# A long convolution with a feed-forward layer: first chunk of k ahead of the filter, bf16 copies in pairs, whole sine tables

## The chip, the core and the metric

The kernel runs on one core of a Trainium2 chip. The metric is the device time of one execution in microseconds (us); lower is better. The core has five engines with a queue each: TensorE (PE in the profile; its weight loads are PEld), VectorE (DVE), ScalarE (ACT), GpSimd (POOL) and SyncE (SP), which issues most DMAs.

## What is computed

```
# q, k, v, x: (1, 2048, 512); shift_k: (512, 4); ssm_k: (512, 2048); all bf16
k_shift = sum over t of k_pad[:, t:t+S, :] * shift_k[:, 3-t]      # four taps per channel
kv  = k_shift * v
y   = irfft(rfft(kv, 2S) * rfft(ssm_k, 2S))[:S] + kv * ssm_D       # long causal convolution
h   = x + layernorm(x) * y                                         # x is q
out = h + relu(layernorm(h) @ w1) @ w2                             # 512 -> 1376 -> 512
```

## The kernel before

The convolution is done as a discrete Fourier transform in two stages of matrix products. Everything up to about 45 us belongs to the part that the change touches; after it come the spectra of the filter and of kv, their product, the inverse transform and the feed-forward layer, with no edit.

**Loads.** SyncE's queue issues `wsh` (the taps), then `sk` (ssm_k, 2 MB, L97), then for each of four chunks of 512 positions a transposing load of k into `kT` (L110) and one of v into `vT` (L111). Each waits its turn in that queue.

**Tables.** GpSimd writes index ramps (L140 to L149). `_turns` (L42) makes of them, in two VectorE instructions, the angles of a table, and a Sin activation on ScalarE makes the table: `cs` (sine, L166) at once, in two instructions of 128x2048, and `cc` (cosine) in slices of four rows, two instructions of 128x256 after each `group_k` (L273). `cn`, the negated sine, is made of `cs` by GpSimd in eight pieces (L192). `f1hi` and `f1lo` are the small first-stage table in two bf16 parts. `wdiag`, made by GpSimd (L195), holds for each channel group and tap a 128x128 matrix with the tap's factors on the diagonal.

**Rows.** `to_rows` (L200) turns eight columns of 128 x 128 with TensorE transposes into one PSUM tile `pst` and copies it (VectorE for D, ScalarE for A, L210 and L208) into `kfl` for ssm_k, later into `xfl` for kv. `pst`, the tap products `pkv` and the first-stage tiles `ps` all come from one ring of eight PSUM slots (tag "ps"): the ninth tile waits until the first is read.

**Rounds.** `taps(u)` (L260) makes the four tap products for chunk u // 4 and channel group u % 4 in one PSUM tile, and VectorE multiplies it with v into `kvx` (L267), which lies in the bytes of `sk`. `stage1` (L213) multiplies rows of `kfl` with `f1hi` and `f1lo` (32-row products, four row groups side by side, 16 quads in a call) and copies the four tiles out. `group_k(gb)` is stage 1 for the filter and a slice of `cc`. The order is written out by hand: `taps(0)`, then seven times `group_k(gb)` and two `taps`, then `taps(15)` and `group_k(7)`. Then `to_rows` makes `xfl` of `kvx`, and eight rounds of `spectrum_k` (twice) and `stage1` on `xfl` follow.

Of the kernel before, what the change touches and what calls it, by code (L numbers as in the profile page):

```python
# [8 lines left out]
ACT = mybir.ActivationFunctionType  # L9
ALU = mybir.AluOpType  # L10
BF16 = mybir.dt.bfloat16
F32 = mybir.dt.float32
F32R = mybir.dt.float32r
I32 = mybir.dt.int32
PSUM = bass.MemoryType.PSUM
P = 128
# [25 lines left out]
def _turns(nc, out, r, col, M, quarter):  # L42

    nc.vector.tensor_scalar(out=out, in0=r, scalar1=col, scalar2=float(M // 2 + (M // 4 if quarter else 0)),
                            op0=ALU.mult, op1=ALU.add)
    nc.vector.tensor_single_scalar(out=out, in_=out, scalar=M - 1, op=ALU.bitwise_and)
# [10 lines left out]
def kernel(  # L57
# [13 lines left out]
    nc = tc.nc  # L71
    _, S, D = A_q.shape
    DFF = B_w1.shape[1]
    KS = A_shift_k.shape[1]
    assert S == 2048 and D == 512 and KS == 4, "kernel is specialised to S=2048, D=512, ks=4"
    NT = 16
    DC = D // P
    NFC = (DFF + P - 1) // P
    x_d, k_d, v_d, out_d = A_q[0], A_k[0], A_v[0], out[0]
# [5 lines left out]
    consts = pl.push("consts")  # L85
    slotA = pl.push("slotA")
    vp = pl.push("vp")
    early = pl.push("early")
    wp = pl.push("wp", side="right")
    kvp = pl.push("kvp", side="right")  # L90
    psum = pl.push("psF", bufs=8, space=PSUM)


    wsh = consts.tile([P, DC, KS], BF16, name="wsh")
    nc.sync.dma_start(out=wsh[:], in_=A_shift_k.rearrange("(r p) j -> p r j", p=P))
    sk = early.tile([P, DC, S], BF16, name="sk")
    nc.sync.dma_start(out=sk[:], in_=A_ssm_k.rearrange("(c p) t -> p c t", p=P))  # L97
    d0 = early.tile([P, DC, 64], BF16, name="d0")
    for dp in range(2):
        src = bass.AP(tensor=A_ssm_D.tensor, offset=A_ssm_D.offset + 64 * dp, ap=[[0, 64], [P, DC], [1, 64]])  # L100
        nc.scalar.dma_start(out=d0[64 * dp:64 * dp + 64, :, :], in_=src)
    CH = 512
    vTs = [vp.tile([P, DC, CH], BF16, name=f"vT{c}") for c in range(4)]
    kT = kvp.tile([P, DC, 16 + S], BF16, name="kT")
    wdiag = kvp.tile([P, DC, KS, P], BF16, name="wdiag")

    nc.vector.memset(kT[:, :, 0:16], 0.0)
    for c in range(4):
        ts = slice(CH * c, CH * c + CH)
        nc.sync.dma_start_transpose(out=kT[:, :, 16 + CH * c:16 + CH * c + CH], in_=k_d[ts, :])  # L110
        nc.sync.dma_start_transpose(out=vTs[c][:], in_=v_d[ts, :])  # L111


    TURN = 2.0 * math.pi * SIN_SHRINK
# [14 lines left out]
    def _sin(out, turns, M, neg=False):  # L129
# [4 lines left out]
    ident = consts.tile([P, P], BF16, name="ident")  # L134
    nc.gpsimd.memset(ident[:], 0.0)
    nc.gpsimd.affine_select(out=ident[:], in_=ident[:], compare_op=ALU.not_equal, fill=1.0,
                            base=0, pattern=[[-1, P]], channel_multiplier=1)
    n2i = early.tile([P, 1], I32, name="n2i")
    for s in range(0, P, 64):
        nc.gpsimd.iota(n2i[s:s + 64, :], pattern=[[0, 1]], base=0, channel_multiplier=1)  # L140
    r2 = early.tile([P, 32, 64], I32, name="w_r")
    nc.gpsimd.iota(r2[:], pattern=[[2, 32], [128, 64]], base=1, channel_multiplier=0)
    n1i = early.tile([P, 1], I32, name="n1i")
    for s in range(0, P, 32):
        nc.gpsimd.iota(n1i[s:s + 32, :], pattern=[[0, 1]], base=0, channel_multiplier=1)
# [1 line left out]
    nc.gpsimd.iota(r1[:], pattern=[[2, 32]], base=1, channel_multiplier=0)  # L147
    r3 = early.tile([P, 64], I32, name="dm_r")
    nc.gpsimd.iota(r3[:], pattern=[[1, 64]], base=0, channel_multiplier=0)  # L149
    n1c = early.tile([P, 1], F32, name="n1c")  # L150
    n2c = early.tile([P, 1], F32, name="n2c")
    nc.vector.tensor_copy(out=n2c[:], in_=n2i[:])


    cc = wp.tile([P, 32, P], F32R, name="c2c")
    cs = wp.tile([P, 32, P], F32R, name="c2s")
    cn = wp.tile([P, 32, P], F32R, name="c2n")

    def table(dst, turns, ks=slice(0, 32)):
        for dp in range(2):  # L160
            nc.scalar.activation(out=dst[:, ks, 64 * dp:64 * dp + 64], in_=turns[:, ks, :], func=ACT.Sin,
                                 scale=hsc[:, dp:dp + 1], bias=hbi[:, dp:dp + 1])

    tsn = early.tile([P, 32, 64], I32, name="w_ts")
    _turns(nc, tsn[:], r2[:], n2c[:], 8192, False)
    table(cs, tsn)  # L166
    nc.vector.tensor_copy(out=n1c[:], in_=n1i[:])

    t1 = early.tile([P, 64], I32, name="f1_t")
    _turns(nc, t1[:, 0:32], r1[:], n1c[:], 128, True)  # L170
# [7 lines left out]
    _turns(nc, t3[:, 1, :], r3[:], n2c[:], 64, False)  # L178
    dsc = early.tile([P, 2, 64], F32, name="dm_f")
    _sin(dsc[:], t3[:], 64)  # L180
    _turns(nc, r2[:], r2[:], n2c[:], 8192, True)
    f1hi = consts.tile([P, 64], BF16, name="f1_hi")
    nc.vector.tensor_copy(out=f1hi[:], in_=f1f[:])
    f1d = early.tile([P, 64], F32, name="f1_d")
# [1 line left out]
    f1lo = consts.tile([P, 64], BF16, name="f1_lo")  # L186
    nc.vector.tensor_copy(out=f1lo[:], in_=f1d[:])

    dtab = consts.tile([P, 8, DC, 8], BF16, name="dtab")
    for h in range(8):  # L190
        hs = slice(4 * h, 4 * h + 4)
        nc.gpsimd.tensor_single_scalar(out=cn[:, hs, :], in_=cs[:, hs, :].bitcast(F32), scalar=-1.0, op=ALU.mult)  # L192
        if h == 0:
            for rg in range(DC):
                nc.gpsimd.tensor_tensor(out=wdiag[:, rg, :, :], in0=ident[:].unsqueeze(1).to_broadcast([P, KS, P]),  # L195
                                        in1=wsh[:, rg, :].unsqueeze(2).to_broadcast([P, KS, P]), op=ALU.mult)
            nc.gpsimd.tensor_copy(out=dtab[:], in_=d0[:].rearrange("p r (o g) -> p o r g", g=8))


    def to_rows(cols, q, fl, eng):  # L200
        pst = psum.tile([P, 8, P], BF16, tag="ps", name="pst")
        for i in range(8):
            nc.tensor.transpose(out=pst[:, i, :], in_=cols(8 * q + i), identity=ident[:])  # L203
        copy(eng, fl[:, :, :, 8 * q:8 * q + 8], pst[:].rearrange("p i (d g) -> p g d i", d=2))

    def copy(eng, o, i):
        if eng == "A":
            nc.scalar.copy(out=o, in_=i)  # L208
        else:
            nc.vector.tensor_copy(out=o, in_=i)  # L210


    def stage1(gb, fl, a_out, engs, parts=1):  # L213
        n = 8 // parts
        for h in range(parts):
            pss = [psum.tile([P, n, 64], F32, tag="ps", name=f"ps1_{r}") for r in range(4)]
            for gi in range(n):
                for f, first in ((f1hi, True), (f1lo, False)):
                    for rg in range(4):
                        rows = slice(32 * rg, 32 * rg + 32)  # L220
                        nc.tensor.matmul(out=pss[rg][:, gi, :],  # L221
                                         lhsT=fl[rows, 8 * gb + n * h + gi, :, :].rearrange("p d n -> p (d n)"),
                                         rhs=f[rows, :], start=first, stop=not first, tile_position=(32 * rg, 0))
            for rg in range(4):
                copy(engs[(4 * gb + rg) % len(engs)], a_out(gb, 8 * rg + n * h, n),
                     pss[rg][:].rearrange("p g c -> p c g"))
# [12 lines left out]
                             skip_group_check=True)  # L239


    kfl = early.tile([P, 64, 2, 64], BF16, name="kfl")
    skv = sk[:].rearrange("p c (a b) -> p c a b", b=64)
    for q in range(8):
        to_rows(lambda n: skv[:, :, :, n], q, kfl, "DADADADA"[q])

    dre = consts.tile([P, 2, P], F32R, name="dre")
    dim = consts.tile([P, 2, P], F32R, name="dim")
# [5 lines left out]
    a1k = a1[:].rearrange("p (c j) -> p c j", j=256)  # L254
    a1x = a1[:].rearrange("p (o c j) -> p o c j", o=8, j=32)


    kvx = sk[:].rearrange("p c t -> p (c t)").rearrange("p (h r a l) -> p h r a l", h=16, r=DC, l=4)

    def taps(u):  # L260
        c, rg = divmod(u, DC)
        ps = psum.tile([P, CH], F32, tag="ps", name="pkv")
        for j in range(KS):
            nc.tensor.matmul(out=ps[:], lhsT=wdiag[:, rg, j, :], rhs=kT[:, rg, CH * c + 16 - j:CH * c + CH + 16 - j],  # L264
                             start=(j == 0), stop=(j == KS - 1))
        split = "p (a h l) -> p a h l"
        nc.vector.tensor_tensor(out=kvx[:, :, rg, 8 * c:8 * c + 8, :].rearrange("p h a l -> p a h l"),  # L267
                                in0=ps[:].rearrange(split, h=16, l=4),
                                in1=vTs[c][:, rg, :].rearrange(split, h=16, l=4), op=ALU.mult)

    def group_k(gb):
        stage1(gb, kfl, lambda o, j, n: a1k[:, :, 32 * o + j:32 * o + j + n], "ADAADADA")
        table(cc, r2, slice(4 * gb, 4 * gb + 4))  # L273

    taps(0)
    for gb in range(7):
        group_k(gb)
        taps(2 * gb + 1)
        taps(2 * gb + 2)
    taps(15)  # L280
    group_k(7)
    for pq in halves:
        for dst, rho, blk, sgn in ((dre, 0, 0, 1.0), (dre, 1, 1, 1.0), (dim, 0, 1, -1.0), (dim, 1, 0, 1.0)):
            nc.gpsimd.tensor_single_scalar(out=dst[pq, rho, pq], in_=dsc[pq, blk, :], scalar=sgn / 2048, op=ALU.mult)
    pl.pop("kvp")
    xfp = pl.push("xfp", side="right")
    xfl = xfp.tile([P, 64, 2, 64], BF16, name="xfl")
    kvc = kvx.rearrange("p h r a l -> p h (r a) l")
    for q in range(8):
        to_rows(lambda n: kvc[:, n // 4, :, n % 4], q, xfl, "ADADADAD"[q])  # L290
    pl.pop("early")
    pl.pop("vp")
    slotB = pl.push("slotB")
# [20 lines left out]
    psum = pl.push("psP", bufs=2, space=PSUM)  # L314
# [69 lines left out]
    psum = pl.push("psI", bufs=8, space=PSUM)  # L384
# [30 lines left out]
    for b in range(32):  # L415
        ps = psum.tile([P, 2, 2 * P], F32, tag="ps", name="psi1")
        m0 = 16 * (b % 4) + 2 * (b // 4)
        for i in range(2):
            m = 2 * b + i
            for c, d in ((0, dre), (1, dim)):  # L420
                nc.tensor.matmul(out=ps[:, i, :], lhsT=kf[:, c, 4 * m:4 * m + 4, :].rearrange("p r k -> p (r k)"),  # L421
                                 rhs=d[:].rearrange("p a b -> p (a b)"), start=(c == 0), stop=(c == 1))
        dst = bp[:, m0:m0 + 2, :, :, :].rearrange("p g a b c -> p g (a b c)")
# [149 lines left out]
    psum = pl.push("psM", bufs=3, space=PSUM)  # L573
# [51 lines left out]
```

## Time and profile before

| | |
|---|---|
| median of 13 runs | 222.65 us (221.7 to 223.8) |
| profiled execution, its time | 223.72 us |
| profiled execution, span on the core | 221.9 us |
| PE busy, share of the span | 198.4 us, 89% |
| DVE busy, share of the span | 149.9 us, 68% |
| ACT busy, share of the span | 132.6 us, 60% |
| POOL busy, share of the span | 72.3 us, 33% |
| granted TensorE clock in every slice of the first 100 us | 1.00 |
| TensorE products of ssm_k's transposes begin | 10.29 us |
| transposes of kvx begin | 38.27 us |

Times in the profile are microseconds from the start of the span unless they are marked ns. In a row of the timeline stand start, length, engine, line, operation, output and inputs, count and in brackets the idle time before it with what ended it. In a row of the groups stand, after the first bar, busy us and mean ns of one instruction, and after the second the engine's idle time before them with its releaser. A q after an engine's name means its queue of DMA issues. The granted clock is the share of TensorE's clock that a throttle let through; the durations show the rest.

### The profile page before, as it was taken

The page shows a single profiled execution, that of the slowest core. Times are in us where ns is not written, and L with a number is a line of the kernel's source. Part 1 is how long each engine was busy: PE and PEld are TensorE (multiplying, and loading weights), DVE is VectorE, ACT ScalarE, POOL GpSimd, SP SyncE. Part 2 cuts the span into 40 slices and gives each one's busy share as a digit, 9 for nine tenths or more (in the row PEclk, how much of TensorE's full clock was granted, in tenths as well). Part 3 has the DMA queues.
Part 4 walks back from the last instruction along what each step waited for, and adds up shares of the span by engine and source line. Part 5 has one row for each costly group of instructions (what it writes and reads, how often), then busy time and mean ns, then how long its engine had stood idle before and what let it go on. Part 6 is the DMA issues. An engine that isn't in the chain of part 4 may idle for free.

```text
span 221.9 us, 7269 instructions
## 1 busy us (share of the span) xinstructions
PE 198.4 (89%) x3092; PEld 137.9 (62%) x3111; DVE 149.9 (68%) x299; ACT 132.6 (60%) x252; POOL 72.3 (33%) x103
## 2 busy tenths in 40 slices
PE   0199699989979999989988799999999999999993
PEld 0194355989968999969976578544444444444452
DVE  4988878989988999966877779751973257130031
ACT  2858967978885888868974879203650066206500
POOL 8399940000018999978300120220022002000000
PEclk9999999999999999999999999999999999999999
DMA  4999940000000000029990000232013110421012
GB/s 154 317 225 195 175 93 4 1 3 6 3 3 3 1 0 3 1 82 227 275 303 9 3 3 3 41 68 63 24 28 80 41 47 4 95 60 38 0 44 53
DMA packets 30384, 15.41 MB, mean 69 GB/s; under 512 B 25520, under 2 KB 29072, under 8 KB 30224
## 3 DMA queue, kind: packets, MB, share of 16 engines
q1 hardware_dynamic: 29520, 14.76, 28.8%
q8 instruction: 24, 0.39, 0.7%
q10 hardware_dynamic: 832, 0.20, 0.4%
q14 instruction: 8, 0.07, 0.1%
HBM read 7.08 MB, written 2.10 MB: 41 GB/s over the span
## 4 chain that ended last, share of the span: by engine, by line
PE 74%; DVE 10%; DMA 5%; issue 4%; ACT 3%; POOL 2%; SPq 1%; DVEq 0%
PE ps2m L540 14%; PE ps1m L528 13%; PE psi L421 7%; PE psy L347 6%; PE pkv L264 6%; PE pz L454 5%; PE pst L203 5%; PE ps L221 4%; DMA sk<-in_A_ssm_k_dram 4%; PE ps2k L236 4%; DVE st L479 4%; PE u L236 4%; PE u L238 3%; PE ps2k L238 3%; POOL rstd L475 2%
## 5 line engine op out<-in xcount | busy, mean ns | idle before, releaser
L530 ACT ACTIVATE h1T<-ps1m 128x512 bf16<-128x512 f32 (+3 forms) x55 | 27.4, 514 | 21.2 <-PE ps1m L528 20.3
L528 PE MATMUL ps1m<-hlnT,w 128*128 128x512 bf16 (+3 forms) x219 | 39.5, 336 | 0.3
L540 PE MATMUL ps2m<-w,h1T 128*128 128x512 bf16 (+3 forms) x177 | 38.9, 366 | 0.7 <-issue 0.3
L542 DVE TENSOR_TENSOR o<-ps2m,xh 128x512 bf16<-128x512 f32 (+1 forms) x17 | 11.1, 659 | 38.1 <-PE ps2m L540 32.8
L528 PEld LDWEIGHTS <-w 128*128 128x128 bf16 (+1 forms) x220 | 21.8, 100 | 17.6 <-issue 1.4
L540 PEld LDWEIGHTS <-h1T 128*128 128x128 bf16 (+1 forms) x187 | 17.6, 98 | 21.2 <-issue 3.1
L337 DVE TENSOR_TENSOR t<-u,kf 128x704 fp32r<-128x704 f32 x32 | 26.7, 886 | 3.0 <-ACT usb L333 2.7
L337 POOL TENSOR_TENSOR t<-usb,kf 128x320 fp32r<-128x320 f32 x32 | 28.2, 919 | 1.3 <-ACT usb L333 1.0
L465 ACT CAST zt<-pz 128x512 bf16<-128x512 f32 x16 | 8.4, 594 | 30.3 <-PE pz L454 30.3
L454 PE MATMUL pz<-bp,ecore 32*32 32x128 f32 x1024 | 23.4, 384 | 2.8 <-issue 1.8
L474 POOL TENSOR_SCALAR rstd<-mv 128x4 f32<-128x4 f32 (+1 forms) x7 | 1.6, 232 | 70.7 <-DVE mv L481 70.7
L208 ACT CAST a<-ps 128x512 fp32r<-128x512 f32 (+1 forms) x38 | 19.4, 569 | 4.6 <-PE ps L221 4.5
L454 PEld LDWEIGHTS pz<-bp,ecore 32*32 32x32 f32 x1024 | 14.5, 103 | 10.5 <-issue 6.3
L210 DVE CAST a<-ps 128x512 fp32r<-128x512 f32 (+1 forms) x30 | 18.4, 651 | 2.4 <-PE ps L221 2.4
L203 PE MATMUL pst<-ident,sk 128*128 128x128 bf16 x128 | 10.1, 248 | 10.5 <-DMA sk<-in_A_ssm_k_dram 10.3
L208 ACT CAST kf<-psy 128x512 fp32r<-128x512 f32 x30 | 17.4, 640 | 1.8 <-PE psy L347 0.3
L479 DVE BATCH_NORM_STATS2 st<-xh 128x6 f32<-128x512 bf16 x28 | 17.3, 676 | 0.0
L264 PE MATMUL pkv<-kT,wdiag 128*128 128x512 bf16 x56 | 14.8, 381 | 2.1 <-issue 1.7
L203 PEld LDWEIGHTS <-sk 128*128 128x128 bf16 x128 | 9.8, 152 | 10.6 <-DMA sk<-in_A_ssm_k_dram 10.3
L421 PE MATMUL psi<-dre,kf 128*128 128x256 f32 x64 | 15.5, 284 | 0.9 <-ACT kf L208 0.9
L347 PE MATMUL psy<-t,ipos 128*128 128x512 f32 x48 | 15.8, 391 | 0.0
L421 PE MATMUL psi<-dim,kf 128*128 128x256 f32 x64 | 15.4, 283 | 0.0
(111 smaller groups left out, 387.4 us busy)
## 6 DMA issues: line engine op xcount, KB each, us to landing
sk<-in_A_ssm_k_dram SPq DMA_DIRECT2D x1, 2048.0 KB, 9.0
out_dram<-o SPq DMA_DIRECT2D x58, 32.0 KB, 1.6
xh<-in_A_q_dram SPq DMA_DIRECT2D x4, 384.0 KB, 6.8
w<-in_B_w_dram SPq DMA_DIRECT2D x1, 1376.0 KB, 12.8
w<-in_B_w_dram SPq DMA_DIRECT2D x1, 1280.0 KB, 15.9
xh<-in_A_q_dram SPq DMA_DIRECT2D x4, 128.0 KB, 2.8
hlnT<-hln SPq DMA_TRANSPOSE x12, 2.4
w<-in_B_w_dram SPq DMA_DIRECT2D x1, 96.0 KB, 15.6
```

What stands on the lines that cost most here:

```text
L203: nc.tensor.transpose(out=pst[:, i, :], in_=cols(8 * q + i), identity=ident[:])
L208: nc.scalar.copy(out=o, in_=i)
L210: nc.vector.tensor_copy(out=o, in_=i)
L264: nc.tensor.matmul(out=ps[:], lhsT=wdiag[:, rg, j, :], rhs=kT[:, rg, CH * c + 16 - j:CH * c + CH + 16 - j], start=(j == 0), stop=(j == KS ...
L337: eng.tensor_tensor(out=t[:, :, j, :], in0=in0.unsqueeze(1).to_broadcast([P, 2, n, 2]), in1=kfr[:, :, j, ks], op=ALU.mult)
L347: nc.tensor.matmul(out=psy[:], lhsT=m_[:], rhs=t_.rearrange("p j k -> p (j k)"), start=first, stop=not first)
L421: nc.tensor.matmul(out=ps[:, i, :], lhsT=kf[:, c, 4 * m:4 * m + 4, :].rearrange("p r k -> p (r k)"), rhs=d[:].rearrange("p a b -> p (a b)" ...
L454: nc.tensor.matmul(out=pz[32 * a:32 * a + 32, r4, l4, :], lhsT=ecore[rows, rho, n2, :], rhs=rhs, start=(rho == 0), stop=(rho == 1), tile_p ...
L479: nc.vector.bn_stats(out=st[:, t % 4, :], in_=xh[:, t, :])
L528: nc.tensor.matmul(out=ps1[:fsz, :], lhsT=w1[:, c, fc * P:fc * P + fsz], rhs=hlnTs[sc][:, c, part], start=(c == 0), stop=(c == DC - 1))
L530: nc.scalar.activation(out=h1s[sc][:fsz, fc, part], in_=ps1[:fsz, :], func=ACT.Relu)
L540: nc.tensor.matmul(out=ps2[:], lhsT=h1s[sc][:ksz, fc, i * P:(i + 1) * P], rhs=w2[:ksz, fc, ds], start=(fc == 0), stop=(fc == NFC - 1))
```

## The change

- k's first chunk is issued ahead of ssm_k, v's first chunk behind it; the other chunks follow in the old order.
- ssm_k loads into a new tile `pre` in slot A, where the angles of the sine table also lie; `kvx` gets a tile of its own.
- Eleven products of a tile of ones are written to a PSUM tile that nobody reads, at the head of TensorE's queue; then `taps` 0 to 3. Their products with v (`times_v`) stand on VectorE behind the second tile of `kfl`.
- `wdiag` moves from GpSimd to VectorE, ahead of the small tables; the long ramp comes last on GpSimd. `cs` is made after the small tables, and `cc` in two whole halves: one ahead of `kfl`'s tiles, one behind them.
- `kfl` and `xfl` hold channels in pairs; `to_rows` copies on VectorE as int32 words with a bitwise or by zero, on ScalarE in two halves; the engine letters change (six of eight tiles on VectorE). Stage 1's weights then have a step of two elements.
- The eight rounds hold twelve `taps`, in turns two and one, ahead of each `group_k`, whose copies go three to ScalarE and one to VectorE ("AADAAADA").

```diff
+    for _ in range(11):
+        nc.tensor.matmul(out=warm[:], lhsT=wz[:, 0:P], rhs=wz[:], start=True, stop=True)
     nc.vector.memset(kT[:, :, 0:16], 0.0)
-    for c in range(4):
+    for c, src in ((0, "k"), (0, "s"), (0, "v"), (1, "k"), (1, "v"), (2, "k"), (2, "v"), (3, "k"), (3, "v")):
...
+    for rg in range(DC):
+        nc.vector.tensor_tensor(out=wdiag[:, rg, :, :], in0=ident[:].unsqueeze(1).to_broadcast([P, KS, P]),
+                                in1=wsh[:, rg, :].unsqueeze(2).to_broadcast([P, KS, P]), op=ALU.mult)
...
-    _turns(nc, r2[:], r2[:], n2c[:], 8192, True)
+    tsn = pre[:, 4096:6144].rearrange("p (k n) -> p k n", n=64)
+    _turns(nc, tsn, r2[:], n2c[:], 8192, False)
+    table(cs, tsn)
...
+    _turns(nc, r2[:], r2[:], n2c[:], 8192, True)
+    table(cc, r2[:], (0,))
...
-        copy(eng, fl[:, :, :, 8 * q:8 * q + 8], pst[:].rearrange("p i (d g) -> p g d i", d=2))
+        qs = slice(8 * q, 8 * q + 8)
+        if eng == "D":
+
+            nc.vector.tensor_single_scalar(out=fl[:].rearrange("p g d n c -> p g d (n c)").bitcast(I32)[:, :, :, qs],
+                                           in_=pst[:].bitcast(I32).rearrange("p i (d g) -> p g d i", d=2),
+                                           scalar=0, op=ALU.bitwise_or)
+        else:
+            for d in range(2):
+                nc.scalar.copy(out=fl[:, :, d, qs, :],
+                               in_=pst[:, :, 64 * d:64 * d + 64].rearrange("p i (g c) -> p g i c", c=2))
...
-                                         lhsT=fl[rows, 8 * gb + n * h + gi, :, :].rearrange("p d n -> p (d n)"),
+                                         lhsT=fl[rows, (8 * gb + n * h + gi) // 2, :, :, gi % 2].rearrange("p d n -> p (d n)"),
...
-        stage1(gb, kfl, lambda o, j, n: a1k[:, :, 32 * o + j:32 * o + j + n], "ADAADADA")
-        table(cc, r2, slice(4 * gb, 4 * gb + 4))
-
-    taps(0)
-    for gb in range(7):
+        stage1(gb, kfl, lambda o, j, n: a1k[:, :, 32 * o + j:32 * o + j + n], "AADAAADA")
+
+    first = [taps(u) for u in range(4)]
+
+    kfl = early.tile([P, 32, 2, 64, 2], BF16, name="kfl")
+    skv = skf.rearrange("p (c a b) -> p c a b", c=DC, b=64)
+    for q in range(8):
+        to_rows(lambda n: skv[:, :, :, n], q, kfl, "DDDDADDA"[q])
+        if q == 1:
+            for u, ps in first:
+                times_v(u, ps)
+    table(cc, r2[:], (1,))
...
+    for gb in range(8):
+        for u in ((4, 5), (6,), (7, 8), (9,), (10, 11), (12,), (13, 14), (15,))[gb]:
+            times_v(*taps(u))
         group_k(gb)
-        taps(2 * gb + 1)
-        taps(2 * gb + 2)
-    taps(15)
-    group_k(7)
...
-        to_rows(lambda n: kvc[:, n // 4, :, n % 4], q, xfl, "ADADADAD"[q])
+        to_rows(lambda n: kvc[:, n // 4, :, n % 4], q, xfl, "DDADDADD"[q])
```

## The prediction

> **What bounds the kernel now.** I read the chain of waits first, in order of time, to see which work ends last in the stretch that the change touches (0 to 45 us of a span of 221.9 us).
>
> ```profile
> 1.25 8.99 DMA sk<-in_A_ssm_k_dram
> 10.29 6.38 PE pst L203 x64
> 16.70 1.02 ACT kfl L208
> 17.77 0.68 PE ps L221 x64
> 18.45 0.32 PE pkv L264
> 18.82 1.46 PE pkv L264 x6
> ...
> 26.12 1.70 issue
> ...
> 38.27 3.77 PE pst L203 x64
> ```
>
> Columns are start, length, what. The kernel does nothing for 10.29 us until ssm_k (sk) has landed, transposes it (64 products), evicts the last tile, and then TensorE sets the pace: a round of `group_k` and two `taps` repeats every 2.45 us (0.61 us for 64 small products of L221, 8 tap products at 0.23 us). At 26.12 TensorE loses 1.70 us in which it waits for nothing that the profile shows. At 38.27 the second set of transposes, of kvx, begins. I call that moment the milestone: everything after it is the same work on the same engines, so what the change gains there it keeps, unless a later step becomes slower. Next the timeline of the first 17 us, for the durations and the order in each queue.
>
> ```profile
> 1.79 8.27 SPq L110 DMA_TRANSPOSE kT<-in_A_k_dram  x1
> ...
> 3.56 2.83 POOL L145 IOTA n1i<- 32x1 int32 x4
> ...
> 6.23 4.08 ACT L161 ACTIVATE c2s<-w_ts,hbi,hsc 128x2048 fp32r<-128x2048 int32 x2 [2.81 <-DVE w_ts L46]
> ...
> 8.20 1.28 DVE L44 TENSOR_SCALAR w_r<-w_r,n2c 128x2048 int32<-128x2048 int32 x1
> 9.52 1.23 DVE L46 TENSOR_SCALAR w_r<-w_r 128x2048 int32<-128x2048 int32 x1
> ...
> 10.11 2.01 SPq L111 DMA_TRANSPOSE vT<-in_A_v_dram  x1
> ...
> 12.28 1.01 ACT L208 COPY kfl<-pst 128x1024 bf16<-128x1024 bf16 x1 [1.24 <-PE pst L203]
> ...
> 13.80 1.01 ACT L208 COPY kfl<-pst 128x1024 bf16<-128x1024 bf16 x1 [0.51 <-PE pst L203]
> ...
> 15.25 1.01 ACT L208 COPY kfl<-pst 128x1024 bf16<-128x1024 bf16 x1 [0.43 <-PE pst L203]
> ...
> 16.70 1.01 ACT L208 COPY kfl<-pst 128x1024 bf16<-128x1024 bf16 x1 [0.44 <-PE pst L203]
> ```
>
> SyncE's queue shows that k's first transposing load sat 8.27 us at the queue behind sk. It landed 10.6 us after its issue, at 12.4; v's first landed 4.5 us after 10.11, at 14.6. ScalarE's evictions wait for TensorE, so the transposes were the limit there. VectorE was through with its tables at 10.8, long before they counted.
>
> The groups by shape in the first 45 us (busy us, mean ns, idle before) give the price of an eviction.
>
> ```profile
> L267 DVE TENSOR_TENSOR sk<-pkv,vT 128x512 bf16<-128x512 f32 x16 | 10.9, 690 | 3.6 <-PE pkv L264 3.6
> L208 ACT CAST a<-ps 128x512 fp32r<-128x512 f32 x20 | 10.6, 592 | 4.3 <-PE ps L221 4.3
> ...
> L210 DVE CAST a<-ps 128x512 fp32r<-128x512 f32 x12 | 7.9, 688 | 0.3 <-PE ps L221 0.3
> ```
>
> **The loads.** k's first chunk is issued at 1.25. An unblocked transposing load took 2.0 us to issue, and about 2.4 us more to land: 5.7. Then sk is issued at 3.3; its own 9.0 us give 12.3, and if it moves only after k's chunk, some 7 us from 5.7 give 12.7. I take 12.5, 2.2 us later than now. v's first chunk, queued behind it, lands 2.2 us after sk, as k's does now, at 14.7 (4.5 us after sk at worst, 17.0). The sum of the loads is the same, so the last chunks land as before, k's at 28.1 (22.02 + 6.1) and v's at 30.1; the first tap that needs k's last chunk comes at about 30.9 in the new rounds, so neither is late.
>
> **Throwaway products and early taps.** Eleven products of 512 columns run from about 1.2; at the slow pace of the first transposes below (107 ns for 128 columns) each takes 0.43, 4.7 in all, to 5.9, when k's chunk is there: off the path. Four `taps` (16 products) follow; they cost 4 x 0.92 = 3.7 us in front of the wait for sk, instead of 3.7 us in the TensorE-bound rounds. The last wants wdiag complete (7.25, below) and so ends by 9.7; the wait for sk covers them with 2.8 us to spare. This is the real gain.
>
> Here a rule speaks. The Trainium skill, TensorE: Matmul & The Clock Gate, Part 1 (The HAM clock gate), says that TensorE runs at half rate until some 3.4 us of busy time: 107 ns per product of 128 columns, then 56. By that, warm transposes would save 64 x (99.5 - 56) = 2.8 us of their 6.37. The rows say otherwise: the ScalarE evictions above, 16 transposes apart, start 1.52, 1.45 and 1.45 us after one another, 95, 91 and 91 ns per transpose, when TensorE has been busy for 2 to 6 us; only the first sixteen are near 107. The second set, whose weights step by 8 bytes rather than 128, takes 3.77 us, 59 ns each. So the step of the weights holds the first set, and the layout of sk stays. I take 64 x (99.5 - 91) = 0.5 us, and it isn't on the path (next).
>
> **VectorE's list becomes the path.** It now makes wdiag (POOL did), then the small tables, then both 2048-wide tables, and only then evicts. From the rows: n1i ends at 1.6 + 2.8 = 4.45 and n1c at 4.65. Wdiag is 4 products of 128x512; the bf16 products of L501 come 0.335 us apart in the chain of waits, those of L267 0.65; with broadcast operands I take the latter, 2.6 us, to 7.25. The eight small steps take 1.5 as now (6.69 to 8.20), to 8.75. One table's two steps 2.56, to 11.3; f1's three casts 1.42 (10.77 to 12.19), to 12.7; the second table 2.56, to 15.25. Now VectorE holds tiles 0 and 1 of kfl, ready at about 14.4.
>
> The new eviction moves pairs of bf16 as 512 int32 words, where L210 moved 1024 elements in 1.22 us. Its nearest row is the 128x512 CAST at 0.69 (0.66 back to back); below, half of 1.22; above, the old 1.22 if nothing is won. I take 0.66. ScalarE's new form is two copies of 512, 2 x 0.57, against 1.01: a little worse. So: tiles 0, 1 to 16.6; four products with v 4 x 0.66 to 19.2; tiles 2, 3, 5, 6 to 21.8. The products with v stand between the tiles because the PSUM ring has eight slots: tiles 4 to 7 of the transposes reuse the slots of the four early taps. The waits that this adds are TensorE's for those slots (7 us that were once full of work, now idle in part), and VectorE's for v; behind both stand all evictions of kfl, and `group_k(0)` needs every one. `group_k(0)` starts at about 21.8 instead of 17.8. This gives back most of the 3.7 us. The taps 4 and 5 stand before it and fit in while the last tiles are evicted (20.0 to 21.8).
>
> ScalarE: the sine table 11.3 to 15.4, the first half of the cosine to 17.5, tile 4 to 19.3, tile 7 to 21.2, the second half of the cosine (2.09) to 23.3. The first eviction of `group_k(0)` on ScalarE is over at 23.9, and TensorE wants its slot at 21.8 + 0.61 + 0.92 = 23.3: 0.5 us lost. The negated sine on POOL runs 15.4 to 27.7 and is wanted at about 40: free.
>
> **The rounds.** From 21.8: 8 x 0.61 + 10 taps x 0.92 = 14.1, with the 0.5 lost and 0.15 for the last product with v the milestone is at 36.5, against 38.27: 1.8 us won. ScalarE has 24 evictions x 0.52 = 12.5 from 23.3, VectorE 20 steps x 0.66 = 13.2 from 21.8: both under TensorE, not by much. That sum has no stall such as 26.12; if it returns whole, 1.7 of it goes. It fell where SyncE's last v load hung for 3.68 us and the DMA engines stood nearly still for a microsecond; with the same loads at the same hour it may or may not.
>
> **xfl.** The transposes bind at 3.77 us, and `group_k`'s twin waits 0.4 + 0.2 us today for the evictions. VectorE's six at 0.66 and ScalarE's two at 1.14 end before that: 0.3 us won.
>
> **The layout in pairs.** Stage 1 now loads weights with a step of 4 bytes. Four row groups load side by side, and four products start every 31 ns, which 16 quads of each stage pay. The trace has no such load. From below: nothing, since a contiguous load fits within 31 ns. From above: a step of 8 bytes fits within 59 ns, so up to 28 ns a quad, 256 quads, 7 us. [...] I take nothing.
>
> **Sum.** 1.8 + 0.3 = 2.1 us off the profiled execution: its span 221.9 becomes 219.8, and with the 1.8 us around it its 223.7 becomes 221.6. That execution is 1.07 above the median of the runs; so 222.65 - 2.1 = 220.5. About 0.3% (0.7 us) is what a measurement can tell from no change.
>
> **Rivals.**
> 1. VectorE's list is shorter than I made it: wdiag at 0.335 saves 1.3 us, the casts without POOL beside them 0.7. Both are in the rows' bounds; the milestone is then at 34.5 and the time 218.5. Chance 0.25.
> 2. The stall of 1.7 us comes back, or v's first chunk lands at 17 and the list is longer: 0 to 0.7 us won, about 222.2. For it: the same DMA load at the same time. Chance 0.15.
> 3. Slower: the 4-byte step of stage 1's weights costs. It sits in all 16 calls, on TensorE, which binds in both halves. 16 ns a quad (the 8-byte load showed 114 ns against 98 for contiguous wdiag) make 256 x 16 = 4.1 us, and 222.65 - 2.1 + 4.1 = 224.7. It decides against the change from 2.1 us / 256 = 8 ns, a pace over 39 ns. Chance 0.13.
> 4. TensorE's clock falls in its gaps (12.5 to 21.8 is half idle). The products in `taps` 4 and 5 double and the first round with them: 2 us, no change, 222.6. The longest gap is about 2.5 us. Chance 0.07.
>
> My own case has 0.40 (219.5 to 221.9). Together: faster 0.68, within 0.15, slower 0.17. The range, 218.2 to 224.2, leaves out the ends of rivals 1 and 3.
>
> **What would show it.** sk's landing near 12.5 and v's near 14.7; VectorE busy without a gap from 4.5 to 21.8; the evictions L221 at 0.66; `group_k(0)` at 21.8; the second transposes at 36.5 with quads at 31 ns. I am wrong if quads slow down, if TensorE's tap products exceed 0.23 us after 20, or if VectorE is not the last to finish before `group_k(0)`.

## The result and the profile after

The changed kernel takes 220.4 us (median of 11 runs, 219.36 to 221.91) against 223.39 us for the kernel before (48 runs, among them those beside the changed kernel). The ratio is 0.9877, 95% interval 0.9854 to 0.9901: 1.2% faster. Its profiled execution took 221.41 us with a span of 219.6 us, 2.3 us shorter than before. The forecast was 220.5, from a kernel before of 222.65: a ratio of 0.990, just above the interval. The total agrees; several of its steps don't, and in the two profiled executions most of the gain is stops of TensorE that got shorter or went away.

The chain of waits of the changed kernel (start, length, what) up to the second transposes, which begin at 36.91 instead of 38.27:

```profile
1.26 2.28 SPq L121
...
4.21 7.74 SPq L123
...
11.99 2.07 SPq L121
...
14.10 2.38 SPq L123
...
16.52 3.96 SPq L121
...
20.52 5.85 DMA vT<-in_A_v_dram
...
26.46 0.70 DVE kvx L278
...
28.25 1.46 PE pkv L271 x6
...
31.29 0.35 PE ps L244 x32
31.64 0.64 issue
32.28 0.41 PE ps L244 x32
...
36.91 3.77 PE pst L217 x64
```

Before, ssm_k's landing and TensorE made up this stretch. Now it is SyncE's queue of transposing loads up to 26.4, when v's third chunk lands: 20.52 + 5.85. Only then TensorE takes over. At 31.64 it stops for 0.64 us inside a run of like products, where it waits for nothing that the profile shows; the stop of this kind in the kernel before, at 26.12, was 1.70 us long. The waits of the first 45 us (us in all, times, longest) say who suffers:

```profile
DVE kvx L278 <- DMA vT<-in_A_v_dram: 4.0, 3, 1.8
PEld L217 <- DMA pre<-in_A_ssm_k_dram: 3.2, 1, 3.2
...
PE ps L244 <- DVE kvx L278: 0.9, 2, 0.7
```

VectorE waits three times for v; its queue and the ring of PSUM tiles pass part of that on to TensorE. The timeline shows the rest of the predicted steps:

```profile
1.66 0.65 POOL L155 IOTA n1i<- 32x1 int32 x4
...
2.71 2.50 DVE L167 TENSOR_TENSOR wdiag<-ident,wsh 128x512 bf16<-128x512 bf16 x4 [0.22 <-DMA wsh<-in_A_shift_k_dram]
...
10.99 1.23 DVE L46 TENSOR_SCALAR w_r<-w_r 128x2048 int32<-128x2048 int32 x1
...
12.25 6.37 PE L217 MATMUL pst<-ident,pre 128*128 128x128 bf16 x64 [2.71 <-DMA pre<-in_A_ssm_k_dram]
...
13.38 0.69 DVE L221 TENSOR_SCALAR kfl<-pst 128x512 int32<-128x512 int32 x1 [1.17 <-PE pst L217]
14.24 0.69 DVE L221 TENSOR_SCALAR kfl<-pst 128x512 int32<-128x512 int32 x1 [0.16 <-PE pst L217]
```

VectorE is through with its tables at 12.2, ssm_k lands at the same time, and then VectorE waits for TensorE (1.17 us), not the other way round. The 64 transposes take 6.37 us, as before to the hundredth. `group_k(0)` starts at 20.28.

In this document M is the start of kvx's transposes (38.27 before, 36.91 after), and U the first product of `u` after the eight rounds on `xfl` (66.4 before, 63.8 after). From U to the end of the span the two differ by 0.3 us (155.5 and 155.8). That is a balance of opposite differences. In the changed kernel's profile, and not in the one before, the granted clock fell to half in the feed-forward layer:

```profile
124.45:127.75 3.30, 3.30 (x75) 2.13 (x44) 3.30 (x11) 2.48 (x5) 0.00 (x0) 0.50 0.02 5
```

(The columns are those of the stretches under e1 below; the clock is the third number from the end.) The stretch around it, from 122.5 to 128.8, is 1.2 us longer than its twin before, and other stretches are 1.0 us shorter. Among all kernels below, whose work behind U is the same, the stretch from U to the end takes 154.0 to 155.8 us.

### The profile page after: what moved, and what is told of

Read it like the earlier page. It is cut to its first block, busy times and chain, and to the rows that moved or that the text cites. A ratio compares the mean times of both kernels' runs of the same rounds, so it can differ in the third digit from the quotient of the medians.

```text
span 219.6 us, 7281 instructions
## 1 busy us (share of the span) xinstructions
PE 203.1 (92%) x3103; PEld 139.9 (64%) x3122; DVE 147.7 (67%) x304; ACT 128.0 (58%) x242; POOL 66.0 (30%) x99
## 4 chain that ended last, share of the span: by engine, by line
PE 78%; SPq 9%; ACT 5%; DMA 3%; issue 2%; DVE 2%; ACTq 0%; DVEq 0%
PE ps2m L568 17%; PE ps1m L556 16%; PE pz L482 8%; PE psi L449 7%; PE psy L375 6%; SPq L123 5%; PE ps2k L259 4%; SPq L121 4%; PE ps L244 4%; PE ps2k L261 3%; PE u L259 3%; PE u L261 3%; DMA vT<-in_A_v_dram 3%; PE pkv L271 2%; PE pst L217 2%
## 5 line engine op out<-in xcount | busy, mean ns | idle before, releaser
L556 PE MATMUL ps1m<-hlnT,w 128*128 128x512 bf16 (+3 forms) x219 | 40.4, 343 | 0.3
L558 ACT ACTIVATE h1T<-ps1m 128x512 bf16<-128x512 f32 (+3 forms) x55 | 27.6, 513 | 21.8 <-PE ps1m L556 21.0
L556 PEld LDWEIGHTS <-w 128*128 128x128 bf16 (+1 forms) x220 | 22.3, 102 | 17.9 <-issue 1.1
L482 PE MATMUL pz<-bp,ecore 32*32 32x128 f32 x1024 | 22.5, 384 | 2.0 <-issue 1.1
L231 ACT CAST a<-ps 128x512 fp32r<-128x512 f32 (+1 forms) x42 | 21.2, 572 | 4.3 <-PE ps L244 4.3
L233 DVE CAST a<-ps 128x512 fp32r<-128x512 f32 (+1 forms) x26 | 16.0, 645 | 1.9 <-PE ps L244 1.9
L449 PE MATMUL psi<-dre,kf 128*128 128x256 f32 x64 | 15.5, 284 | 0.9 <-ACT kf L231 0.9
L209 POOL TENSOR_SCALAR c2n<-c2s 128x512 fp32r<-128x512 f32 x8 | 11.9, 1536 | 8.8 <-ACT c2s L177 8.8
L278 DVE TENSOR_TENSOR kvx<-pkv,vT 128x512 bf16<-128x512 f32 x16 | 10.6, 687 | 4.8 <-DMA vT<-in_A_v_dram 4.0
```

What stands on the lines that cost most here:

```text
L482: nc.tensor.matmul(out=pz[32 * a:32 * a + 32, r4, l4, :], lhsT=ecore[rows, rho, n2, :], rhs=rhs, start=(rho == 0), stop=(rho == 1), tile_p ...
L556: nc.tensor.matmul(out=ps1[:fsz, :], lhsT=w1[:, c, fc * P:fc * P + fsz], rhs=hlnTs[sc][:, c, part], start=(c == 0), stop=(c == DC - 1))
L558: nc.scalar.activation(out=h1s[sc][:fsz, fc, part], in_=ps1[:fsz, :], func=ACT.Relu)
```

## The experiments

Twelve kernels. In the table T is the start of ssm_k's transposes, the ratio is to the kernel before on the same chip, and an edit is to the changed kernel unless it says "before". A stop is one of TensorE before M, inside a run of like products, for nothing that the profile shows. T, M, U and the stops come from one profiled execution of each kernel; only the ratio has an interval.

| kernel | ratio (95% interval) | T | T to M | M to U | stops |
|---|---|---|---|---|---|
| before | 1 | 10.29 | 27.98 | 28.1 | 1.70 |
| changed | 0.9877 (0.9854 to 0.9901) | 12.25 | 24.66 | 26.9 | 0.64 |
| e1, no throwaway products | 0.9893 (0.983 to 0.9955) | 13.14 | 25.46 | 26.9 | 1.41, 1.17 |
| e2, throwaway products until ssm_k lands | 0.9881 (0.9816 to 0.9945) | 12.48 | 24.53 | 26.9 | 0.73 |
| e3, no pairs | 0.9878 (0.9823 to 0.9933) | 12.86 | 24.20 | 27.6 | 0.54 |
| e4, one chunk of v | 0.9799 (0.9747 to 0.9852) | 12.93 | 22.99 | 26.9 | none |
| e5, cosine in slices | 0.9972 (0.9935 to 1.001) | 12.85 | 26.99 | 27.0 | 2.13 |
| e6, taps back in the rounds | 1.0052 (1.002 to 1.0083) | 13.27 | 27.33 | 26.9 | 0.63 |
| e7, before with k first | 1.014 (1.007 to 1.0209) | 12.25 | 27.85 | 28.1 | 1.49 |
| e8, before with pairs | 0.9957 (0.993 to 0.9985) | 10.0 | 27.79 | 26.9 | 1.17 |
| e9, taps a round later | 0.9888 (0.9862 to 0.9914) | 13.25 | 24.55 | 26.9 | 1.34 |
| e10, products with v behind | 0.9977 (0.995 to 1.0004) | 12.9 | 26.28 | 26.9 | 0.66 |
| e11, throwaway products of 16 columns | 0.9857 (0.983 to 0.9884) | 12.38 | 24.08 | 26.9 | 0.69 |
| e12, e9 and e10 | 1.0089 (1.0058 to 1.012) | 12.86 | 28.99 | 26.9 | 1.63 |

T varies by 1 us among kernels with the same loads up to it (12.25 to 13.27), so within a microsecond the stretches from T to M and from M to U say more than M.

My theory for the result, after reading the two traces: the early taps pay, TensorE's transposes (not VectorE) start the rounds, and late chunks of v give about 1.7 us back. The rival: the pairs and the clock carry the gain, and v's waits are idle time that costs nothing.

### e1, e2 and e11: the throwaway products

```diff
-    for _ in range(11):
-        nc.tensor.matmul(out=warm[:], lhsT=wz[:, 0:P], rhs=wz[:], start=True, stop=True)
```

> The eleven throwaway products and their tile are left out. Theory A (the granted clock had fallen back to 0.50 by 12 us, so they buy nothing for the transposes, and the loads of v set the rounds): the transposes of ssm_k still take 6.4 us, the transposes of kvx begin at 36.9 +- 0.4, the time is that of the changed kernel, 220.4 +- 0.5. The four early taps run at the slow pace (0.43 us a product, 7 us instead of 3.6) and still end by 13.5, so at most 1 us is lost. Theory B (the products do raise the clock for what follows): transposes longer, kvx's transposes 1 us or more later, 221.5 or more.

e2 puts thirteen such products behind the early taps:

```diff
     first = [taps(u) for u in range(4)]
+    for _ in range(13):
+        nc.tensor.matmul(out=warm[:], lhsT=wz[:, 0:P], rhs=wz[:], start=True, stop=True)
```

> Thirteen more throwaway products behind the four early taps, so that TensorE is busy until ssm_k lands and the granted clock stays at 1.00. By the clock rule (half rate, then full rate) the 64 transposes fall from 6.4 us to 3.6 to 3.8. By the step of the weights (128 bytes) they stay at 91 ns each, 5.8 us. In both cases group_k(0) starts 0.5 us earlier or more, but if the loads of v set the rounds the transposes of kvx stay at 36.9 +- 0.4 and the time at 220.4 +- 0.5; if TensorE sets them, 0.5 to 2.7 us are won.

e11 keeps eleven, with 16 columns each:

```diff
-        nc.tensor.matmul(out=warm[:], lhsT=wz[:, 0:P], rhs=wz[:], start=True, stop=True)
+        nc.tensor.matmul(out=warm[:, 0:16], lhsT=wz[:, 0:P], rhs=wz[:, 0:16], start=True, stop=True)
```

> The eleven throwaway products with 16 columns in place of 512: as many instructions, hardly any work. Without them TensorE lost 1.4 and about 1.3 us in waits for nothing that the profile shows, at 24.1 and in the round after. If those hang on where the instructions lie in TensorE's stream, they stay away here and kvx's transposes begin at 36.9 +- 0.5; if they hang on the early work, they begin at 38.6 as without the products.

Stretches of the changed kernel, and of e2 below it (us, then busy us and count of PE, PEld, DVE, ACT, POOL; after those the granted clock, DMA share, GB/s):

```profile
9.50:11.50 2.00, 0.04 (x1) 0.00 (x0) 1.93 (x4) 2.00 (x2) 0.00 (x0) 1.00 1.15 375
...
12.50:13.50 1.00, 1.00 (x12) 1.00 (x12) 0.12 (x1) 1.00 (x2) 0.10 (x1) 0.50 1.13 254
13.50:14.50 1.00, 1.00 (x12) 1.00 (x11) 0.84 (x2) 1.00 (x1) 1.00 (x1) 0.50 1.11 153
...
15.50:16.50 1.00, 1.00 (x14) 1.00 (x14) 1.00 (x3) 0.00 (x0) 1.00 (x1) 1.00 1.72 279
```

```profile
12.50:13.50 1.00, 1.00 (x11) 1.00 (x12) 0.03 (x1) 1.00 (x2) 0.09 (x1) 1.00 1.27 290
13.50:14.50 1.00, 1.00 (x14) 1.00 (x13) 0.97 (x2) 1.00 (x1) 1.00 (x1) 1.00 1.02 177
14.50:15.50 1.00, 1.00 (x14) 1.00 (x13) 1.00 (x3) 0.92 (x1) 1.00 (x3) 1.00 1.20 242
```

The count in a window includes products that only overlap it. In the changed kernel TensorE is idle from 9.54, and by 12.5 the granted clock is 0.50; it is 1.00 again by 15.5, while transposes alone are running. The throwaway products raised it for work that doesn't need it, and it is gone when ssm_k comes. In e2 it is 1.00 throughout, and the 64 transposes still take 6.00 us, 94 ns each, against 6.37. The clock rule of the prediction (56 ns when warm) would have made them 3.6; the 91 ns that the prediction read from the rows holds. From T to M e2 gains 0.13 us over the changed kernel: nothing.

e11 says what the products are worth as work. Its early taps run at the slow pace (6.19 to 12.54 instead of 5.92 to 9.54) and so fill the wait for ssm_k by themselves; TensorE never rests, and the transposes take 5.92 us. M is 36.46 and the ratio 0.9857, the lowest of all kernels that compute everything, though its interval overlaps the changed kernel's.

e1, without the instructions, was expected at 36.9. Its ratio can't be told from the changed kernel's, but in its profile (of the slowest of its four runs, 222.69 us against 221.27 to 221.91) M is 38.60. From its chain of waits:

```profile
23.76 0.38 PE pkv L266
24.14 1.41 issue
25.55 1.26 PE pkv L266 x5
...
28.39 0.54 PE ps L239 x55
28.93 1.17 issue
30.10 0.26 PE ps L239 x9
```

Twice TensorE stops in the middle of a run of like products, where no semaphore stands, and waits for nothing that the profile shows: 2.58 us. It is the same kind of stop as at 26.12 in the kernel before. e11, with the same early work at the same slow pace but with the instructions there, has none of 1 us or more before M, only one of 0.69. So the stops go with the place in TensorE's instruction stream, not with the early work.

The traces tie the stops to a queue. `prof LABEL --dma` lists a DMA queue q8, kind "instruction", with 24 packets of 16 KB over the span. TensorE has 6225 products and weight loads in the changed kernel, which would be 63 bytes for each; so I take q8, an estimate by count, for TensorE's instruction stream. A packet is under way from 25.40 to 26.34 in the kernel before, from 30.04 to 31.00 in the changed one, and from 23.14 to 24.26 and 27.76 to 28.73 in e1. All 14 stops of the table end 1.2 to 1.6 us after the end of such a packet. While one is under way, the transposing loads hardly move. This is the kernel before in the windows 24.3:25.3, 25.5:26.5 and 26.75:27.75:

```profile
DMA packets 778, 0.20 MB, mean 199 GB/s; under 512 B 778, under 2 KB 778, under 8 KB 778
...
DMA packets 108, 0.03 MB, mean 28 GB/s; under 512 B 108, under 2 KB 108, under 8 KB 108
...
DMA packets 737, 0.18 MB, mean 181 GB/s; under 512 B 737, under 2 KB 737, under 8 KB 737
```

A transposing load normally holds SyncE's queue for 1.7 to 2.7 us. All 23 longer holds (2.9 to 4.0 us, the load right behind ssm_k left out) have the start of such a packet inside them, and none of the 69 shorter ones has. So the stops and the long holds, which make chunks late, have one thing in common. Not every packet brings a stop (e4 has packets from 24.40 and 28.16 and none), no run moved them alone, and why TensorE runs dry at one and not at another stays open.

### e3 and e8: the pairs

e3 undoes the pairs in the changed kernel, e8 puts them alone into the kernel before (layout, copies and the engine letters of the tiles).

```diff
-            nc.vector.tensor_single_scalar(out=fl[:].rearrange("p g d n c -> p g d (n c)").bitcast(I32)[:, :, :, qs],
...
+        copy(eng, fl[:, :, :, 8 * q:8 * q + 8], pst[:].rearrange("p i (d g) -> p g d i", d=2))
```

> The pairs are undone in the changed kernel: old layout, old copies, old engine letters (four tiles each on VectorE and ScalarE); all else as changed. VectorE's copies are 1.22 us again. If kfl's copies hide behind the transposes of ssm_k, group_k(0) starts at 20.3 to 21.5 and kvx's transposes at 36.9 to 37.5; behind them 0.3 us of wait for xfl's copies comes back, 220.7 to 221.3. If the pairs carry the gain, the time goes back to 222 or more.

> The kernel before with the pairs alone: layout, copies as int32 words or in halves, and the engine letters of the changed kernel for the tiles. If the transposes of ssm_k and of kvx set the pace, the evictions hide: the time is that of the kernel before, -0.3 to +0.3 us, with quads at 31 ns. If the pairs are a part of the gain, 1 us or more below it.

e8 was expected to change nothing, and is 0.43% faster (0.15 to 0.7). From T to M it is like the kernel before (27.79 and 27.98). The gain lies behind M: 26.9 against 28.1 us. The chain of waits of the kernel before and that of e8 in the first rounds on `xfl`:

```profile
42.98 0.19 ACT xfl L208
43.17 0.58 issue
43.76 0.70 ACT kf L303
...
44.49 0.65 PE ps L221 x61
...
47.25 0.59 PE ps L221 x61
47.84 0.50 issue
48.34 0.21 PE ps L221 x3
```

```profile
43.52 0.62 PE ps L230 x64
44.13 0.32 PE ps2k L245
...
46.24 0.62 PE ps L230 x64
46.86 0.32 PE ps2k L245
```

Before, the first stage 1 on `xfl` waits for the copies of `xfl` and what is queued behind them; 61 of its 64 products start at 44.49, 6.2 us after M. In e8 they start at 43.52, 5.7 us after M. Then the kernel before stops for another 0.50 us in the second stage 1, behind 61 of 64 products, again for nothing that the profile shows. That stop is in e7 too, in the same place (61), and in e3, whose stream has 22 more instructions ahead of it, ten products earlier (51). None of the kernels with pairs has it, not even e8, whose TensorE stream is the same as before. The stop too ends 1.2 to 1.5 us after a packet of q8 in all three kernels that have it. So 0.5 us is copies, 0.5 us a stop of the stream that goes away with the pairs for a reason that stays open.

In e3 the time can't be told from the changed kernel's; its stretch from M to U is 0.7 us longer. The pairs are worth 0.4% in the kernel before, and in the changed one less than three rounds can show.

### e4, e9, e10 and e12: the loads of v

e4 leaves work out: three of v's chunks aren't loaded, and all products use the first.

```diff
-    for c, src in ((0, "k"), (0, "s"), (0, "v"), (1, "k"), (1, "v"), (2, "k"), (2, "v"), (3, "k"), (3, "v")):
+    for c, src in ((0, "k"), (0, "s"), (0, "v"), (1, "k"), (2, "k"), (3, "k")):
...
-                                in1=vTs[c][:, rg, :].rearrange(split, h=16, l=4), op=ALU.mult)
+                                in1=vTs[0][:, rg, :].rearrange(split, h=16, l=4), op=ALU.mult)
```

> Work left out: only v's first chunk is loaded, and all products use it. If the loads of v set the rounds, VectorE's waits for them (4.0 us) go and k's chunks land earlier too: kvx's transposes begin at 35.0 to 35.5 and the time falls by 1.4 to 1.9 us, to about 218.8. If TensorE, ScalarE or the ring of PSUM tiles sets them, they begin at 36.9 and the time stays at 220.4 +- 0.5.

From T to M it takes 22.99 us, 1.67 less than the changed kernel, and the ratio is 0.8 points lower; the two intervals just fail to overlap. No wait for v is left in its list. But no stop is left either, where the changed kernel has one of 0.64. So the late chunks cost about 1.0 us, and 1.67 at most. (M itself is 35.92, 0.99 earlier, because ssm_k landed 0.7 us later. The other 1.3 us by which its span of 217.3 is shorter lie behind U, where nothing was edited.)

Two ways to win it back with all the work:

```diff
-        for u in ((4, 5), (6,), (7, 8), (9,), (10, 11), (12,), (13, 14), (15,))[gb]:
+        for u in ((4, 5), (6,), (7,), (8,), (9, 10), (11, 12), (13,), (14, 15))[gb]:
```

> The changed kernel with the twelve taps one round later where v's third chunk is not there yet: (4,5) (6) (7) (8) (9,10) (11,12) (13) (14,15). If the loads of v set the rounds, their demand moves toward their landing and 0.5 to 1.3 us are won: kvx's transposes at 35.6 to 36.4, time 0.2 to 0.6% below the changed kernel. If not, no change.

```diff
-            times_v(*taps(u))
         group_k(gb)
+        for u, ps in held:
+            times_v(u, ps)
```

> The changed kernel with each round's products with v behind that round's copies on VectorE, so that a wait for v holds no copy. If the loads of v hold the rounds through VectorE's order, TensorE's waits for PSUM tiles fall and 0.5 to 1.5 us are won, kvx's transposes at 35.4 to 36.4. But the last product with v then stands behind the last copy, 0.7 us later: net 0 to 0.8. If the ring of PSUM tiles holds them anyway, no change or 0.5 us slower.

> Both: taps later and products with v behind the copies. If the loads of v set the rounds, TensorE waits least here: kvx's transposes at 35.2 to 36.0, 0.4 to 0.8% below the changed kernel. If ScalarE's 24 evictions set them (12.5 us from 21.6 on, 34.1 at best), not below 35.5.

All three failed. e9's waits for v are gone from its list, but its chain shows that the microsecond went elsewhere:

```profile
26.57 0.48 PE ps L244 x48
27.05 1.34 issue
28.39 0.30 PE ps L244 x16
```

Again a stop inside a run of like products. It lies where SyncE's queue holds v's last load for 3.34 us (24.91 to 28.25); the stop of the kernel before (26.12 to 27.82) lay inside the hold of its last load too (24.17 to 27.85). A long hold is on one or two of the last four loads in every full set, with a packet of q8 inside, and whether it shows as a late chunk, as a stop of TensorE or as both varies. So e9 proves nothing against the theory and wins nothing: 24.55 us from T to M.

e10 and e12 are slower than the changed kernel by 1.0 and 2.1 points. The last products with v now stand behind the last copies, and kvx's transposes wait for them; from e10's waits:

```profile
PE pst L217 <- DVE kvx L278: 1.5, 1, 1.5
...
DVE a L233 <- issue: 1.4, 1, 1.4
```

The expectation allowed 0.7 us for that; it took 1.5 in e10 and 2.1 in e12, and VectorE stopped besides. In e12 two things come on top that the edit didn't aim at, a stop of TensorE of 1.63 us and, behind it, a stretch at half clock, in which six tap products took 2.39 us instead of 1.46:

```profile
27.16 1.63 issue
...
29.46 2.39 PE pkv L271 x6
```

```profile
29.80:33.20 3.40, 3.40 (x71) 1.51 (x70) 0.96 (x3) 1.24 (x3) 0.00 (x0) 0.51 0.02 5
```

### e5 to e7: the other parts alone

e5 makes the cosine in slices after each `group_k` again; e6 puts the first four taps back into the rounds; e7 moves the load alone.

```diff
-    table(cc, r2[:], (0,))
-    table(cc, r2[:], (1,))
...
+        for dp in range(2):
+            nc.scalar.activation(out=cc[:, 4 * gb:4 * gb + 4, 64 * dp:64 * dp + 64], in_=r2[:, 4 * gb:4 * gb + 4, :], func=ACT.Sin,
```

> The cosine table is made in slices of four rows after each group_k again, as before; all else as changed. ScalarE then carries 24 evictions x 0.52 + 16 slices x 0.55 = 21.3 us in the rounds, which last 16.6 us now. If whole tables are a needed part, ScalarE sets the rounds: from the first eviction at about 21.0 to 42, kvx's transposes 3 us or more later (ring of PSUM tiles), time 223 or more. If the loads of v leave room for it, 36.9 and 220.4 +- 0.5.

```diff
-    first = [taps(u) for u in range(4)]
+    first = []
...
-        for u in ((4, 5), (6,), (7, 8), (9,), (10, 11), (12,), (13, 14), (15,))[gb]:
+        for u in ((0, 1), (2, 3), (4, 5), (6, 7), (8, 9), (10, 11), (12, 13), (14, 15))[gb]:
```

> The four early taps go back into the rounds, two taps in each; k's first chunk still loads first. If the early taps are the gain, TensorE has 3.7 us more in the rounds, of which the waits for v (about 1.9 us at TensorE) swallow a part: kvx's transposes 1.8 to 2.5 us later, at 38.7 to 39.4, time 222.2 to 222.9. If the rounds wait for the loads alone, 36.9 and 220.4 +- 0.5.

e7, to the kernel before:

```diff
-    nc.sync.dma_start(out=sk[:], in_=A_ssm_k.rearrange("(c p) t -> p c t", p=P))
...
         nc.sync.dma_start_transpose(out=kT[:, :, 16 + CH * c:16 + CH * c + CH], in_=k_d[ts, :])
+        if c == 0:
+            nc.sync.dma_start(out=sk[:], in_=A_ssm_k.rearrange("(c p) t -> p c t", p=P))
         nc.sync.dma_start_transpose(out=vTs[c][:], in_=v_d[ts, :])
```

> The kernel before with one edit: k's first chunk is issued ahead of ssm_k. ssm_k lands 2 us later (12.3) and everything behind it follows: kvx's transposes at 39.6 to 40.5 and the time 1.5 to 2 us above the kernel before. This is the price that the early taps have to earn back. If the 1.7 us stall of TensorE goes away with the shift, 0 to 0.5 us above.

e7 gives the price of the reordering: T 1.96 us later, M at 40.10, 1.83 later, and the ratio 1.014 (1.007 to 1.0209), if anything more than the 1.5 to 2 us expected. e6 gives the worth of the early taps: without them the changed kernel is slower than the kernel before (1.0052). From T to M it takes 2.67 us more than the changed kernel, 0.2 more than expected, and no wait for v is left in its rounds: TensorE's own work covers the loads. Its stop is as long as the changed kernel's (0.63 and 0.64), so stops have no part in the 2.67.

e5 loses 0.95 points, 2.3 us from T to M. ScalarE is busy for 16.2 of 19.0 us of its rounds (12.3 of 16.6 in the changed kernel), and from 28.89 to 39.21 the chain stays on it, copies and slices in turn:

```profile
28.89 1.55 ACT a L230 x3
30.45 0.98 ACT c2c L284 x2
```

But before that TensorE stopped for 2.13 us, and behind the stop the clock fell:

```profile
26.70:30.10 3.40, 3.18 (x71) 1.46 (x69) 1.92 (x3) 2.63 (x6) 2.15 (x7) 0.50 1.12 122
```

One of the ten runs, with a mean clock of 0.992 where the others have 0.981 to 0.989, took 220.36 us, no more than the changed kernel. So the slices cost time in most executions; how much of that is ScalarE's load, and how much the stop and the clock, is open.

## Why the prediction was right, and where it wasn't

1. **The loads.** ssm_k at 12.5: measured 12.25. v's first chunk at 14.7: 4.21 + 10.5 = 14.7. But "neither is late" failed: I checked when k's last chunk is wanted, not v's third. It landed at 26.4 (24.7 before) and was wanted at about 24.6; v's last at 32.0 (30.1 before). e4 puts a price of about 1.0 us on it, 1.67 at most.
2. **Throwaway products.** Row against rule was decided rightly: with the clock at 1.00 the transposes take 94 ns each (e2), not 56. That the clock would fall again before T, and that small products do as well (e11), I had not seen. Rival 4 had the fall, but in the rounds; it came in the wait for ssm_k and, ahead of M, touched the transposes alone. That the step of the weights is what makes them slow was read from two rows: no run varied it alone, and the first set also runs while loads land, the second doesn't.
3. **Early taps.** The gain: 3.7 us of work moved, 2.67 us found by e6, against 1.83 us that the later ssm_k costs (e7).
4. **VectorE's list becomes the path.** Wrong. The term that failed is n1i, put at 2.83 us from the old row; it took 0.65, and the list was over at 12.2 instead of 15.25. The casts of f1 took 0.67 in all (9.08 to 9.75), not 1.42. Wdiag was 2.50 (2.6 predicted), the new eviction 0.69 (0.66 to 0.69). So `group_k(0)` waited for the transposes and the taps 4 and 5 behind them, and came at 20.28, not 21.8: 1.5 us to the good. Rival 1 had the shorter list, but not that the transposes would stand right behind it.
5. **The rounds.** Predicted 36.5 - 21.8 = 14.7 us, measured 36.91 - 20.28 = 16.6: 1.9 us to the bad: 0.64 is the stop at 31.64, most of the rest point 1. The 0.5 us for the second half of the cosine is not on the changed kernel's chain, though on those of e1, e4, e9 and e12 (20.45, 2.00 us in e4). Points 4 and 5 cancel: M was 36.91 for 36.5, and 1.36 us were won for 1.8.
6. **xfl.** Predicted 0.3, measured 1.2 from M to U. The mechanism (copies no longer waited for) was right and its size too small: 0.5, and 0.5 from a stop in the second stage 1 that I took for granted.
7. **The 4-byte step.** Free, as assumed: four products of the changed kernel's stage 1 start every 31 ns (20.28 to 20.75 for 16 quads). Rival 3 is out.

The sum, 1.36 + 1.2 less 0.3 behind U, is 2.3 us of span for the 2.1 predicted; two errors of 1.5 and 1.9 us with opposite signs, and a third of 0.9, lie inside it. Rival 2 (the stall returns or v is late) was half of what happened.

The agreement is luck in one more way. The sum for M, 36.5, had no stop in it, and was set against 38.27, which has 1.70 us of stop: of the 1.8 us forecast at M, 1.7 was the stop's going. It shrank to 0.64, and by the two chains of waits 1.06 of the 1.36 us won at M is that. With the 0.5 us behind M, stops are about 1.6 of the 2.3 us of span. Apart from stops, the early taps, the order of the loads and the lists won 0.3 us at M, and the copies 0.5 behind it. The prediction said that the stall may or may not return; it gave no cause for its going, and no run here shortened it alone. Nor were the move of wdiag and the new engine letters of stage 1 tried alone.

## What to carry to other kernels

When work is moved ahead of a load, the rounds that lose it run faster and reach every later load sooner: check each chunk against the new demand, not only the last one. A duration read from an engine that ran beside another (n1i on GpSimd beside VectorE's long integer steps) isn't its duration elsewhere. Work that merely keeps TensorE's clock up is lost if the wait behind it is long enough for the clock to fall; useful work at the slow pace inside the wait did as well. And before a gain is put down to an edit, the stops of both kernels belong in the sum: they move with the number of instructions, and here they outweigh what the edit was made for.

## What the runs showed of the hardware

- The granted clock was 0.50 by 12.5 us after TensorE had been idle since 9.54, and rose to 1.00 after some 3 us of transposes alone (from 12.25; at 1.00 again by 15.5).
- The transposes of ssm_k, whose weights step by 128 bytes, took 91 to 94 ns each at full clock, those of kvx, with 8 bytes, 59 ns. The first ran while loads landed.
- The four n1i ramps on GpSimd took 0.65 us without, and 2.83 us beside VectorE's 128x2048 integer steps. The casts of 128x64 took 0.19 us where GpSimd was idle, and 0.50 and 0.62 us where it wasn't.
- TensorE stopped for 0.4 to 2.1 us inside runs of like products. The place moves with the number of instructions ahead (61 to 51 products for 22 instructions). Each of the 14 stops before M ended 1.2 to 1.6 us after a 16 KB packet of DMA queue q8 (kind "instruction").
- Such a packet took 0.9 to 1.8 us, and the transposing loads nearly stood still beside it (108 packets in 1 us against 778 and 737). All 23 holds of SyncE's queue of 2.9 to 4.0 us have the start of one inside, none of the 69 of 2.7 us or less.
